# A mixture-of-experts feed-forward: a narrower path for experts with up to 192 tokens, and the weights fetched and split on an even schedule

## The chip, the cores and the metric

The program runs on one core of a Trainium2 chip. The metric is the device time of one execution in microseconds (us). The engines are named as the profile names them: PE multiplies matrices, PEld is PE's weight load, DVE and ACT are the vector and the scalar engine, POOL is the general-purpose engine, and SP issues most of the DMAs. An engine runs its own instructions in the order in which they are written and waits for others at semaphores.

## The reference

First a local and global attention over 8 batches of 544 rows, then a feed-forward layer in which a row is computed only where its skip score is positive, by the one of 8 experts that its gate picks.

```python
def reference(**kwargs):
    attn_out = _attn_ref(**attn_kwargs)          # (8, 8, 544, 64)
    x = attn_out.transpose(0, 2, 1, 3).reshape(B * S, H * D)    # (4352, 512)
    return _moe_ref(x=x, **moe_kwargs)

def _moe_ref(x, w_skip, w_gate, w1, w2):         # w1 (8, 512, 1024), w2 (8, 1024, 512)
    out = x.copy()
    do_compute = x @ w_skip > 0
    xc = x[do_compute]
    logits = xc @ w_gate
    e_idx = np.argmax(logits, axis=1)
    probs = softmax(logits)
    gate_w = probs[np.arange(len(xc)), e_idx]
    for e in range(8):
        mask = e_idx == e
        h = np.maximum(xc[mask] @ w1[e], 0.0)
        y[mask] = gate_w[mask, None] * (h @ w2[e])
    out[do_compute] = xc + y
```

With the inputs of the reference the experts 0 to 7 get 395, 171, 153, 289, 173, 371, 253 and 175 rows.

## The kernel before

The attention part fills the first half of the span and writes its rows (`x`) to the output in DRAM; it also appends each computed row's number and gate weight to a list of its expert in DRAM (`lst`). The change leaves it as it is. What follows is the expert part, lines 818 to 1040.

The order of every engine is written out by hand: the code runs under a manual schedule, so instructions stand on each engine as the Python emits them, and a "hook" after each step of a loop says what is slipped in there.

Each expert e handles its rows in a first group of 256 (`GRP`), and the rest, if any, in an extra group.

- `slots` reads the lists of row numbers and gate weights into `lt`, and `index` casts the numbers into `six`. In the first group, rows 2p and 2p+1 of the list go to partition p.
- `gather` (POOL, two indirect DMAs of 128 rows) fetches the rows: `xfirst` and `xsecond` in turn for the first groups, `xmore` for the extra ones.
- `turn_x` transposes them on PE (8 transposes of 128x128) and writes a high part `xh` (ACT) and the remainder `xl` (DVE): each float32 operand is used as a sum of two reduced-precision (`fp32r`) parts, so a product takes three matmuls: high x high, high x low, low x high.
- The up product (L858): for each of the 8 blocks `f` of 128 hidden units, 12 matmuls with 256 moving columns (4 of `w1h` with `xh`, 4 of `w1l` with `xh`, 4 of `w1h` with `xl`) into one of three PSUM banks `ph`; then ACT writes `hh` = relu(ph) and DVE the remainder `hlw`.
- The down product (L874): for each of the 2 token blocks `t` of 128 rows, 24 matmuls with 512 moving columns (per f: `hh` x `w2h`, `hh` x `w2l`, `hlw` x `w2h`) into a bank `py`. `put` then multiplies by the gate weight, adds the row (DVE, L939), and scatters the rows to the output (POOL, L940).
- The hook numbers 0 to 7 are the blocks of the up product, 8 to 15 those of the down product of t=0, 16 to 23 those of t=1.
- After the first group, `If(num > 256)` (L1010) holds the extra group: in full (L858 and L874 again) over 384 rows, else `ffn_half`, which does 128 rows another way (L904, L930). `num` is read from `cni` by all engines (L982).

Weights: expert e+1's two matrices (4 MB) come in 8 chunks of 512 KB (`raw`, six buffers); a `split` casts the chunk to its high part on ACT (L181) and subtracts on DVE (L184). Expert 1's first four chunks are issued on SP and the last four on POOL at hook 9 of expert 0, behind the gathers (`rest`); four of them are split in expert 0 at hooks 4 to 7, the other four in expert 1 at hooks 0 to 3, before expert 2's eight. In expert 1 and after it, the next expert's chunks are split at hooks 4, 5, 6, 8, 9, 11, 13, 15 (expert 1) or 0, 1, 2, 4, 5, 6, 9, 11.

## Time and profile before

| | |
|---|---|
| time, median of 3 runs | 499.26 us (497.95 to 500.41) |
| the profiled execution's own time | 503.73 us |
| its span | 502.0 us |
| mean granted PE clock | 0.986 |
| PE busy | 455.9 us (91%) |
| expert part: first up product to last scatter issued | 245.7 to 493.7 us |

The difference between the profiled execution's time and its span (1.7 us) lies around the program. Times inside the trace are counted from the span's start. A row of the timeline gives start, duration, engine, line, operation, output and inputs, shape and count, and in brackets the idle time of the engine just before it with what ended it. In a row of a window the busy time of each engine is followed by the number of its instructions, then the granted clock, the DMA engines' busy share and the GB/s that they moved.

### The profile page before, as it was taken

What the parts mean: (1) busy time and instruction counts of PE and PEld (TensorE: products, weight loads), DVE (VectorE), ACT (ScalarE), POOL (GpSimd) and SP (SyncE); (2) the same over time, 40 slices, a digit from 0 to 9 for tenths busy, and PEclk for the clock granted to TensorE, in tenths of its full rate; (3) what the DMA queues carried; (4) which work ended last, traced back from release to release, by engine and by line L of the source; (5) the groups of instructions that cost most, each with busy time, mean ns of one, the idle gap of its engine ahead of it and who ended that gap; (6) DMA issues with size and microseconds to landing.
All of it is one profiled execution on the core that took longest, in us unless ns stands there. A gap on an engine that the chain in (4) does not pass through costs nothing. (4 is left out here: it accounts for less than half of the span.)

```text
span 502.0 us, 13663 instructions
## 1 busy us (share of the span) xinstructions
PE 455.9 (91%) x4962; PEld 368.5 (73%) x4962; DVE 298.7 (59%) x1221; ACT 289.6 (58%) x883; POOL 228.2 (45%) x236
## 2 busy tenths in 40 slices
PE   8799999999989998887698999999989999899991
PEld 3576767776666767666696979898968888688881
DVE  6886767877757767784453229684714757047310
ACT  4689999899868887764341208563514545145210
POOL 6656666669864677776246014323202341013300
PEclk9999999999999999999899999999999999899996
DMA  8899898889957788610547308883820949113100
GB/s 252 267 329 262 268 288 279 254 281 219 289 171 244 226 189 255 169 45 2 172 146 216 109 26 268 313 295 121 286 99 10 343 142 327 38 23 131 46 15 17
DMA packets 50545, 93.32 MB, mean 186 GB/s; under 512 B 15596, under 2 KB 19948, under 8 KB 50448
## 3 DMA queue, kind: packets, MB, share of 16 engines
q1 hardware_dynamic: 44624, 81.83, 52.0%
q0 software_dynamic: 5824, 10.25, 6.2%
q8 instruction: 55, 0.90, 0.9%
q14 instruction: 42, 0.34, 0.3%
HBM read 82.91 MB, written 14.67 MB: 194 GB/s over the span
## 5 line engine op out<-in xcount | busy, mean ns | idle before, releaser
L368 ACT ACTIVATE prob<-prob,nmx 128x160 f32<-128x160 f32 x256 | 106.4, 418 | 17.9 <-DVE nmx L363 15.7
L398 POOL TENSOR_TENSOR prob<-prob,inv 128x640 f32<-128x640 f32 x64 | 80.3, 1257 | 61.1 <-DVE ing L428 24.0
L863 ACT ACTIVATE hh<-ph 128x256 fp32r<-128x256 f32 x72 | 27.7, 385 | 83.2 <-PE ph L858 71.8
L940 POOL DMA_INDIRECT out_dram<-yo,six x12 | 12.2, 1018 | 134.6 <-DVE yo L939 116.7
L874 PE MATMUL py<-w2h,hh 128*128 128x512 f32 x144 | 57.2, 397 | 0.0
L874 PE MATMUL py<-w2h,hlw 128*128 128x512 f32 x144 | 56.9, 395 | 0.0
L874 PE MATMUL py<-w2l,hh 128*128 128x512 f32 x144 | 56.7, 394 | 0.0
L351 PE MATMUL pss<-ks,qs 64*64 64x160 f32 x1024 | 51.5, 305 | 3.1 <-DVE nmx L363 1.6
L864 DVE SCALAR_TENSOR_TENSOR hlw<-ph,hh 128x256 fp32r<-128x256 f32 x72 | 30.3, 421 | 32.4 <-ACT hh L863 29.6
L351 PEld LDWEIGHTS pss<-ks,qs 64*64 64x64 f32 x1024 | 34.1, 134 | 20.9 <-issue 15.2
L858 PE MATMUL ph<-xh,w1h 128*128 128x256 f32 x288 | 46.4, 283 | 3.2 <-ACT xh L844 1.5
L482 PEld LDWEIGHTS pv<-ptT,vw 128*64 128x64 f32 x1024 | 39.4, 137 | 13.3 <-issue 3.9
L368 ACT ACTIVATION_READ_ACCUMULATOR prob<-prob,nmx 128x1 f32 x256 | 48.4, 189 | 0.0
L482 PE MATMUL pv<-ptT,vw 128*64 128x64 f32 (+1 forms) x1024 | 44.2, 237 | 3.4 <-ACT ptT L441 1.6
L858 PE MATMUL ph<-xh,w1l 128*128 128x256 f32 x288 | 45.5, 280 | 0.0
L858 PE MATMUL ph<-xl,w1h 128*128 128x256 f32 x288 | 45.4, 280 | 0.0
L858 PEld LDWEIGHTS ph<-xh,w1h 128*128 128x128 f32 x288 | 39.3, 191 | 5.9 <-issue 3.8
L639 POOL DMA_INDIRECT lst<-dat,slu x34 | 34.3, 1008 | 18.0 <-DVE cni L959 9.6
L858 PEld LDWEIGHTS ph<-xh,w1l 128*128 128x128 f32 x288 | 39.1, 190 | 0.0
L858 PEld LDWEIGHTS ph<-xl,w1h 128*128 128x128 f32 x288 | 39.0, 190 | 0.0
L438 PE MATMUL pst<-ident,prob 128*128 128x128 f32 x256 | 36.6, 281 | 2.5 <-POOL prob L398 1.2
L184 DVE TENSOR_TENSOR w1l<-raw,w1h 128x1024 fp32r<-128x1024 f32 x28 | 34.1, 1220 | 6.6 <-ACT w1h L181 4.1
(178 smaller groups left out, 942.3 us busy)
## 6 DMA issues: line engine op xcount, KB each, us to landing
raw<-in_w_dram SPq DMA_DIRECT2D x60, 512.0 KB
vw<-in_v_dram SPq DMA_DIRECT2D x32, 512.0 KB
ks<-in_kT_dram SPq DMA_DIRECT2D x32, 400.0 KB
out_dram<-xr SPq DMA_DIRECT2D x32, 256.0 KB
qs<-in_qT_dram SPq DMA_DIRECT2D x31, 256.0 KB
vgs<-in_vgl_dram SPq DMA_DIRECT2D x32, 64.0 KB
raw<-in_w_dram POOLq DMA_DIRECT2D x4, 512.0 KB
lst<-dat,slu POOLq DMA_INDIRECT x34
```

Of the source, the lines that this page charges most:

```text
L184: eng.tensor_sub(lo, raw, hi.bitcast(F32))
L351: nc.tensor.matmul(banks[odd][head(h ^ odd), j * W:(j + 1) * W], q[head(h), w * QB:(w + 1) * QB], window(k[head(h)], w), start=True, stop= ...
L368: nc.scalar.activation(pt[:, i, :], pt[:, i, :], AF.Exp, bias=nmx[:, i:i + 1], scale=-1.0, accum_out=sums[:, i, 0:1],)
L398: nc.gpsimd.tensor_mul(pt[:, sl, :], pt[:, sl, :], inv[:, sl].unsqueeze(2).to_broadcast([P, 4, W]),)
L438: nc.tensor.transpose(pst[:, i * P:(i + 1) * P], pt[:, 4 * hf + i, 0:KW], ident)
L482: nc.tensor.matmul(pv[head(h), j * 96:j * 96 + n], vv[:, w, head(h)], ptT[:, w, h ^ odd, 0:n], start=j == 0, stop=False, skip_group_check= ...
L639: ins = nc.gpsimd.indirect_dma_start(out=lst, out_offset=bass.IndirectOffsetOnAxis(ap=slu[:, t:t + 1], axis=0), in_=dat[:, bs[j], t - 4 * ...
L858: nc.tensor.matmul(ph[:, 0:GRP], hl[a][:, c, f * P:(f + 1) * P], bb[:, c, :], start=i == 0, stop=i == 3 * NC - 1,)
L863: nc.scalar.activation(hh[:, f, :], ph[:, 0:GRP], AF.Relu)
L864: nc.vector.scalar_tensor_tensor(hlw[:, f, :], ph[:, 0:GRP], 0.0, hh[:, f, :].bitcast(F32), ALU.max, ALU.subtract,)
L874: nc.tensor.matmul(py, a[:, f, ts_], hl[bb][:, f, :], start=f == 0 and i == 0, stop=f == NF - 1 and i == 2,)
L940: ins = nc.gpsimd.indirect_dma_start(out=out, out_offset=bass.IndirectOffsetOnAxis(ap=sidx, axis=0), in_=yo, in_offset=None, bounds_check= ...
```

## The change

It does four things.

1. **A path for up to 192 rows** (`FEW`). From expert 1 on, the up product stands twice, in the two arms of `If(nums[e] > FEW)` (L1128 of the changed kernel), and so does everything after the down product of t=0 (L1141). In the short arm `up_few` does a block f in 8 matmuls: 4 of `w1h` with 384 columns (192 of the high part and 192 of the low part side by side) and 4 of `w1l` with 192. ACT copies the second 192 columns, DVE adds them to the first, and relu and remainder are made from the sum, one block later. Rows 128 to 191 and their remainders then share one block of 128 stationary columns (POOL copies the remainders there, L1135), so that `down_few` does the second token block in 16 matmuls instead of 24, and `leave_few` adds the two halves: one ACT copy, and a second DVE instruction in `put`.
2. **The lists** are read so that rows 0 to 127 are token block 0: two DMAs with 8-byte pieces where one with 16-byte pieces was (experts 1 to 7).
3. **The weights** form one stream over all experts in six fixed buffers; a chunk is issued (`feed`) right after the split that frees a buffer. Expert 1's eight chunks are all split in expert 0 (hooks 4 to 7 and 17 to 20); chunks 4 to 7 are issued on ACT's queue (`early`, hooks 6 to 9) and no longer on POOL's behind the gathers. From expert 1 on the splits are at hooks 0, 2, ... 14; in `up_few` the second one's subtraction is done by POOL.
4. **The next expert's** rows are turned and its count is read at hook 15 and no longer at 16. The high and low parts are halves of one tile.

With the counts above, experts 1, 2, 4 and 7 take the short arms.

PE, where the up product of expert 1 stands; before, the last two of 8 blocks and the first matmul of the down product (`ph` is the result, `xh`, `xl` the rows' parts, `w1h`, `w1l` the weights' parts):

```order
L858 MATMUL ph<-xh_4453,w1h 128x256 x4
L858 MATMUL ph<-xh_4453,w1l 128x256 x4
L858 MATMUL ph<-xl_4454,w1h 128x256 x4
L858 MATMUL ph<-xh_4453,w1h 128x256 x4
L858 MATMUL ph<-xh_4453,w1l 128x256 x4
L858 MATMUL ph<-xl_4454,w1h 128x256 x4
L874 MATMUL py<-w2h,hh 128x512
```

The same place in the changed kernel: the end of the long arm, and the last two blocks of the short one (`x_4458` holds both parts).

```order
L864 MATMUL ph<-x_4458,w1l 128x256 x4
L864 MATMUL ph<-x_4458,w1h 128x256 x4
L1128 UNCONDITIONAL_BRANCH
L883 MATMUL ph<-x_4458,w1h 128x384 x4
L888 MATMUL ph<-x_4458,w1l 128x192 x4
...
L883 MATMUL ph<-x_4458,w1h 128x384 x4
L888 MATMUL ph<-x_4458,w1l 128x192 x4
L1128 UNCONDITIONAL_BRANCH
L916 MATMUL py<-w2h,h_4459 128x512
```

A block went from twelve rows of 256 columns to four of 384 and four of 192 in the short arm, and branches stand around both arms.

ACT in expert 0, from its sixth up block to the read of the counts; before:

```order
L863 ACTIVATE hh<-ph 128x256
L181 CAST w1h<-raw 128x1024
L863 ACTIVATE hh<-ph 128x256
L181 CAST w1h<-raw 128x1024
L863 ACTIVATE hh<-ph 128x256
L181 CAST w1h<-raw 128x1024
L982 TENSOR_LOAD cni
L844 CAST xh_4453<-xt 128x4x128 x2
```

The same place in the changed kernel, from the issue of the fifth chunk, ahead of the eighth up block's relu, on:

```order
L153 DMA raw_4451<-in_w_dram 128x2x512
L869 ACTIVATE h_4459<-ph 128x256
L188 CAST w1h<-raw_4450 128x1024
L153 DMA raw_4452<-in_w_dram 128x2x512
L153 DMA raw_4447<-in_w_dram 128x2x512
L153 DMA raw_4448<-in_w_dram 128x2x512
L188 CAST w2h<-raw_4451 128x1024
L188 CAST w2h<-raw_4452 128x1024
L188 CAST w2h<-raw_4447 128x1024
L188 CAST w2h<-raw_4448 128x1024
L1061 TENSOR_LOAD cni x2
L852 CAST x_4458<-xt 128x4x128 x2
```

Four DMA issues and four casts, each of which waits for its chunk, now stand ahead of the casts of expert 1's rows (`xt` to `x`).

The diff, cut to its core:

```diff
+Q = P // 2
+FEW = P + Q
 ...
     def slots(es, g):
-        if g == 0:
+        if g == 0 and es.start == 0:
             nc.sync.dma_start(
                 lt[:, es, 0].rearrange("p e t c -> p e (t c)"),
                 l3[es, 0:GRP, :].rearrange("e (p t) c -> p e (t c)", t=NSUB),
             )
         else:
             for t in range(NSUB):
+                n0 = g * GRP + t * P
                 nc.sync.dma_start(
-                    lt[:, es, 1, t],
-                    l3[es, GRP + t * P:GRP + (t + 1) * P, :].rearrange("e p c -> p e c"),
+                    lt[:, es, g, t], l3[es, n0:n0 + P, :].rearrange("e p c -> p e c")
                 )
 ...
+    def up_few(e, x2, hook, bank):
+        hl, late = wq[e], []
+        for f in range(NF):
+            ph = bank("ph")
+            fs = slice(f * P, (f + 1) * P)
+            for c in range(NC):
+                nc.tensor.matmul(
+                    ph[:, 0:2 * FEW], hl["w1h"][:, c, fs], x2[:, :, c, 0:FEW],
+                    start=c == 0, stop=False, skip_group_check=True,
+                )
+            for c in range(NC):
+                nc.tensor.matmul(
+                    ph[:, 0:FEW], hl["w1l"][:, c, fs], x2[:, 0, c, 0:FEW],
+                    start=False, stop=c == NC - 1, skip_group_check=True,
+                )
+            hs = fw.tile([P, DM], F32, name="yo")[:, 0:FEW]
+            nc.scalar.copy(hs, ph[:, FEW:2 * FEW])
+            nc.vector.tensor_add(hs, ph[:, 0:FEW], hs)
+            if late:
+                late.pop()()
+            def part(f=f, hs=hs):
+                h, lo = hh[:, f, 0:FEW], hlw[:, f, 0:FEW]
+                nc.scalar.activation(h, hs, AF.Relu)
+                nc.vector.scalar_tensor_tensor(
+                    lo, hs, 0.0, h.bitcast(F32), ALU.max, ALU.subtract
+                )
+            late.append(part)
+            if f == NF - 1:
+                late.pop()()
+            hook(f)
+    def down_few(e, hook, bank):
+        ...
+        for f in range(NF):
+            for i, bb in enumerate(("w2h", "w2l")):
+                nc.tensor.matmul(
+                    py, hh[:, f, P:GRP], hl[bb][:, f, :],
+                    start=f == 0 and i == 0, stop=f == NF - 1 and i == 1,
+                )
+            hook(2 * NF + f)
+        return py
+    def leave_few(py, xg, gate, sidx):
+        ys = fw.tile([P, DM], F32, name="ylast", bufs=1)
+        nc.scalar.copy(ys[0:Q], py[Q:P])
+        put(py, gate(1), xg[:, 1, :], sidx[:, 1:2], None, ys)
 ...
+        else:
+            gate, yo, sidx = gate[0:Q], yo[0:Q], sidx[0:Q]
+            nc.vector.scalar_tensor_tensor(yo, py[0:Q], gate, x[0:Q], ALU.mult, ALU.add)
+            nc.vector.scalar_tensor_tensor(yo, rest[0:Q], gate, yo, ALU.mult, ALU.add)
 ...
-            for _ in range(4):
-                weights[1].load(nc.gpsimd)
 ...
             if e + 1 < E:
                 load_weights(e + 1)
-                for _ in range(8 if e else 4):
-                    weights[e + 1].load()
+                for _ in range((4, 2, 0)[min(e, 2)]):
+                    feed()
 ...
             def split():
                 if e + 1 < E:
-                    weights[e + 1].split(nc.vector)
+                    w = weights[e + 1]
+                    w.split(nc.gpsimd if few and w.done % 4 == 1 else nc.vector)
+                    if e or w.done > NCH // 2:
+                        feed()
             if e == 0:
-                todo = {i: split for i in (4, 5, 6, 7)}
+                todo = {i: split for i in (4, 5, 6, 7, 17, 18, 19, 20)}
+                def early(i):
+                    if 6 <= i < 10:
+                        feed(nc.scalar)
             else:
-                todo = {i: split for i in (0, 1, 2, 4, 5, 6, 9, 11)}
-                todo[16] = nxt
+                todo = {i: split for i in range(0, 16, 2)}
+                todo[15] = nxt
 ...
+                with tc.If(nums[e] > FEW) as many:
+                    up(e, xs[e % 2], hook, ps_s)
+                with many.Else():
+                    up_few(e, xs[e % 2], hook, ps_s)
+                    nc.gpsimd.tensor_copy(hh[:, :, FEW:GRP], hlw[:, :, P:FEW])
+            put(down(e, 0, hook, ps_v), gate(0), xg[:, 0, :], sidx[:, 0:1])
+                with tc.If(nums[e] > FEW) as many:
+                    second()
+                with many.Else():
+                    leave_few(down_few(e, hook, ps_v), xg, gate, sidx)
```

## The prediction

> **What bounds the kernel now.** The page's first lines come first, then a table of windows cut at the steps of the expert part, then the timeline of PE.

> ```profile
> span 502.0 us, 13663 instructions
> PE 455.9 (91%) x4962; PEld 368.5 (73%) x4962; DVE 298.7 (59%) x1221; ACT 289.6 (58%) x883; POOL 228.2 (45%) x236
> L858 PE MATMUL ph<-xh,w1h 128*128 128x256 f32 x288 | 46.4, 283 | 3.2 <-ACT xh L844 1.5
> ```

> The third line tells which groups ran: a group of 256 rows issues 8 x 4 = 32 products of that kind, so 288 are nine groups: eight first groups and one full extra one.

> ```profile
> 274.65:285.96 11.31, 11.31 (x96) 11.31 (x97) 3.75 (x9) 2.69 (x7) 0.45 (x1) 1.00 0.45 162
> 285.96:297.20 11.24, 11.24 (x50) 8.83 (x48) 1.18 (x2) 0.38 (x1) 1.02 (x1) 1.00 0.07 25
> 298.29:309.67 11.38, 11.38 (x96) 11.38 (x97) 9.46 (x13) 9.15 (x14) 6.95 (x6) 1.00 0.55 174
> 309.67:322.10 12.43, 12.16 (x58) 9.71 (x57) 10.11 (x13) 6.60 (x9) 1.02 (x1) 1.00 0.97 354
> 470.00:492.00 22.00, 21.67 (x143) 19.35 (x141) 4.61 (x11) 3.07 (x8) 4.08 (x4) 1.00 0.07 23
> ```

> After length, the columns are PE, PEld, DVE, ACT and POOL busy, granted clock, DMA share, GB/s. The rows are expert 0's extra group (up, down), expert 1 (up; down with the turn of expert 2's rows) and expert 7. PE has no gap, at a full clock, and expert 1's up product takes the same time with DVE and ACT four fifths full as expert 0's with both idle. So PE sets the time here, and what leaves PE leaves the span, as long as the rest keeps up.

> ```profile
> 274.65 0.74 PE L858 MATMUL ph<-xh,w1h 128*128 128x256 f32 x4 [0.78 <-ACT xh L844]
> 285.96 0.40 PE L874 MATMUL py<-w2h,hh 128*128 128x512 f32 x1
> 296.92 0.40 PE L874 MATMUL py<-w2h,hlw 128*128 128x512 f32 x1
> 298.29 0.71 PE L858 MATMUL ph<-xh,w1h 128*128 128x256 f32 x4 [0.97 <-PEq L1016]
> 322.12 0.71 PE L858 MATMUL ph<-xh,w1h 128*128 128x256 f32 x4 [0.29 <-PEq L1010]
> ```

> Durations overlap, so starts count. A 256-column product steps by (285.96 - 274.65)/96 = 0.1178 us; a 512-column one by (296.92 - 285.96)/47 = 0.2332, or 0.456 ns a column (0.460 at 256).

> **The change part by part.** *Fewer products.* 384 columns lie between the two prices: 0.176. For 192 the floor by columns is 0.088; the ceiling is 0.118, since the same weights are loaded for 256 columns at that step. The nearest rows of narrow products:

> ```profile
> 244.42 0.63 PE L837 MATMUL xt<-ident,xfirst 128*128 128x128 f32 x4 [2.13 <-DMA xfirst<-out_dram,six]
> L837 PE MATMUL xt<-ident,xfirst 128*128 128x128 f32 x32 | 4.4, 274 | 3.2 <-DMA xfirst<-out_dram,six 3.2
> ```

> A 128-column transpose steps by (0.63 - 0.274)/3 = 0.119, twice its price by columns: narrow products are held up by something else. I take 0.110, near that row and inside the ceiling. The short up product is then 8 x (4 x 0.176 + 4 x 0.110) = 9.15 for 11.31, a saving of 2.16; the second token block drops 8 of 24 products, 8 x 0.2332 = 1.87. Four experts: 4 x 4.03 = -16.1 (-15.1 with the narrow step at 0.118, -18.9 at 0.088).

> [...] Whether loads or something else make the 0.119 no row here shows.

> *The evacuation of a short block.* Per block ACT has a copy and a relu of 192 columns where a relu was, DVE an addition and the remainder where a remainder was, and at each second block a split.

> ```profile
> L509 ACT COPY xT<-pv 128x256 f32<-128x256 f32 x64 | 20.3, 368 | 9.5 <-PE pv L501 9.4
> L441 ACT COPY ptT<-pst 128x512 f32<-128x512 f32 x32 | 18.2, 568 | 2.8 <-PE pst L438 2.8
> L863 ACT ACTIVATE hh<-ph 128x256 fp32r<-128x256 f32 x72 | 27.7, 385 | 83.2 <-PE ph L858 71.8
> L864 DVE SCALAR_TENSOR_TENSOR hlw<-ph,hh 128x256 fp32r<-128x256 f32 x72 | 30.3, 421 | 32.4 <-ACT hh L863 29.6 <-issue 1.5 <-ACTq L1016 1.0
> L181 ACT CAST w1h<-raw 128x1024 fp32r<-128x1024 f32 x28 | 29.2, 1044 | 0.3 <-DMA raw<-in_w_dram 0.3
> L184 DVE TENSOR_TENSOR w1l<-raw,w1h 128x1024 fp32r<-128x1024 f32 x28 | 34.1, 1220 | 6.6 <-ACT w1h L181 4.1 <-issue 1.5 <-DMA lst<-dat,slu 0.9
> ```

> A column of a copy costs (568 - 368)/256 = 0.78 ns, so 192 columns take 0.32, and I put the relu at 0.33. Two blocks cost ACT 2 x 0.32 + 2 x 0.33 + 1.04 = 2.34 and DVE, at about 0.33 for the addition and 0.36 for the remainder, 2 x 0.69 + 1.22 = 2.60, where PE needs 2 x 1.144 = 2.29. They are at PE's pace or just over, and the two hidden buffers `yo` make copy f+2 wait for remainder f. What pays is slack: three banks, and block 7 is first needed 4.9 us into the down product (7 x 3 x 0.233). If the engines pay whole durations, in this order with 0.06 per hand-over, PE loses 1.2 per expert; if neighbours overlap by 0.1, nothing. Experts 1, 2 and 4 have splits; expert 7 has none. I take 1.5 in all (0 to 4), the middle. `yo` is also what expert 3's extra group scatters just ahead of expert 4; that wait is within the 4.

> *Expert 0.* These rows are POOL's and SP's in expert 0, and PE's wait for the turned rows:

> ```profile
> 261.69 0.38 SPq L106 DMA_DIRECT2D lt<-lst  x1
> 262.12 1.50 SPq L112 DMA_DIRECT2D lt<-lst  x2
> 265.24 0.82 SPq L165 DMA_DIRECT2D raw<-in_w_dram  x2
> 265.78 1.05 POOL L119 DMA_INDIRECT xsecond<-out_dram,six  x1 [7.18 <-issue]
> 270.81 1.29 PE L837 MATMUL xt<-ident,xsecond 128*128 128x128 f32 x8 [1.35 <-DMA xsecond<-out_dram,six]
> 250.00:255.00 5.00, 5.00 (x52) 5.00 (x51) 2.27 (x11) 1.39 (x4) 2.25 (x3) 1.00 0.96 361
> ```

> Lists, then gathers, then PE: it already waits 1.35 and then 0.78 for the cast. Now the lists are one DMA more, with pieces of 8 bytes, and four chunks (2 MB) issued by ACT between hooks 6 and 9 move at the same time; at the last row's 361 GB/s these are 5.8 us. No row shows how lists and gathers share the engines with that. The low end is 0.5: the chunks end before the gathers, and the casts of the rows are only held up by the four splits ahead of them on ACT (4 x 1.04, most of it during the gathers). The high end is 6: the gathers come after all of the chunks. I take +2.5, less than half of the chunks, since the first are under way when the lists are read; range 0.5 to 6. The split of expert 1's last four chunks leaves expert 1 and so costs expert 0's extra group cover it has: DVE 3.75 of 11.31 is taken.

> *POOL and the stream.* In a short arm POOL does one subtraction of 1024:

> ```profile
> L184 POOL TENSOR_TENSOR w1l<-raw,w1h 128x512 fp32r<-128x512 f32 x8 | 10.2, 1270 | 0.0
> 352.71 1.16 POOL L119 DMA_INDIRECT xfirst<-out_dram,six  x1 [0.30 <-issue]
> 345.77 0.72 PE L858 MATMUL ph<-xh,w1h 128*128 128x256 f32 x4
> ```

> It takes 2 x 1.27 = 2.54 and stands behind the gathers, which end 8.1 after an expert's start (352.71 + 1.16 - 345.77), so its buffer and the chunk fed into it are some 10 us late. SP issues in order: later chunks wait behind that one. 4 MB take 11.6 us of a 20 us expert, so the cover holds by some us; if it does not, the next expert's first products wait. +0.5 (0 to 3). Moving the turn from hook 16 to 15 goes past nothing that waits: hook 15 is some 6 us after the gathers' end.

> *The end.* The last scatter waits for DVE:

> ```profile
> 491.71 0.75 DVE L939 SCALAR_TENSOR_TENSOR ylast<-py,lt,xsecond 128x512 f32<-128x512 f32 x1 [4.75 <-PE py L874]
> ```

> Now a copy on ACT (beside DVE's first) and a second such instruction: +0.75 (0.6 to 1.5).

> *The branches.* Seven experts pass two more `If`s, on all engines. PE's waits at the present ones are the 0.97 and 0.29 quoted. Both stand where an expert ends and a count is read; the new ones have their counts early and stand inside running work, between the same expert's products, so I take most as covered: +1 (0 to 13.6, each of 14 at 0.97).

> The sum: -16.1 + 1.5 + 2.5 + 0.5 + 0.75 + 1 = -9.85. The profiled execution's own time is 503.73 (span 502.0 and 1.7 around it), 4.5 above the median of 499.26. On its scale that gives 493.9; taken from the median, **489.4**.

> **The rivals.** *Exposed branches* (slower). Each way into or out of an arm halts the engine as at 298.29, whatever work surrounds it. The price is that row's 0.97, and 14 jumps cost 13.6, 12.6 more than counted: 489.4 + 12.6 = 502.0. It ends above before from ten of the fourteen on (-10.85 without any, 11 x 0.97 = 10.7). For it speaks the 0.97; against it the 0.29 at the next boundary, where PE passes the same kind of `If` with its condition false.

> [...]

> *The lists starve.* The 2 MB on ACT's queue go ahead of lists and gathers in full: 5.8 for what I put at 2.5, and the lists behind the same again: 489.4 + 5.8 = 495.2. For it speaks that PE waits for these gathers today, against it that 5.8 us of transfer, begun at 262, may end by the gathers' start.

> *Narrow fp32r products go at the price of plain float32.* No product of these two-part operands under 256 columns ran. Plain float32 has this row:

> ```profile
> 239.95 0.63 PE L531 MATMUL pr<-idw,xTg 128*128 128x137 f32 x4
> L531 PE MATMUL pr<-idw,xTg 128*128 128x137 f32 x16 | 2.6, 286 | 1.8 <-ACT xr L549 1.8
> ```

> Two records make a product there, (0.63 - 0.286)/3 = 0.115 each, so 137 columns take 0.23 or 1.68 ns a column. 192 then take 0.322, and 4 x 32 x (0.322 - 0.110) = +27.1: 516.5. Against it: 256 and 512 columns cost the same per column, so nothing begins to bend at 256.

> **How the numbers follow.** Forecast 0.70, branches 0.12, lists 0.10, narrow price 0.08. The forecast's own range is 481 to 496: all unknowns at their low ends give -18.9 + 0.5 + 0.6 = -17.8, or 481.5; upwards I let the evacuation and the lists go to their ends (+2.5 and +3.5). For 8 in 10 over all cases, 481 to 500: it takes in the lists and a part of the branches, and leaves out the narrow price. About 0.5% of 499, 2.5 us, is what a measurement can tell from no change. Faster: forecast and most of the lists, with a little of the branches, 0.76. Same: the branches around 499 to 501.8, 0.08. Slower 0.16.

> **What would show it.** In the changed profile PE's short up product should last 9.2 to 9.5 from its first 384-column product to the down product, and the second token block 16 x 0.233 = 3.7. A 192-column step over 0.2 would be the narrow price. DVE's idle time before its additions, and PE's waits for a bank in the short arms, show the evacuation. PE's waits for `xsecond` and for the cast in expert 0, 2.1 together now, should come to about 4.6; over 8 would be the lists. PE idle by its own queue at the new `If`s, each near 1, would be the branches. The forecast fails if expert 1 or 2 waits for chunks, or if the gain on PE returns as waits at these places.

## The result, and the profile after

The changed kernel takes 538.09 us (median of 4 runs, 537.07 to 541.97) where the kernel before takes 498.61 in the same comparison: a ratio of 1.0809 (95% interval 1.0736 to 1.0882), some 40 us slower. Forecast were 489.4 us, in a range of 481 to 500. Here and below a median is over all runs, while a ratio leaves out the executions that ran in a slower state (the profile of *fixed* is of one, so its expert part is left out).

The profiled execution took 537.24, its span is 535.4. The page's first lines:

```profile
span 535.4 us, 13599 instructions
PE 458.4 (86%) x4802; PEld 370.0 (69%) x4802; DVE 311.5 (58%) x1254; ACT 297.6 (56%) x919; POOL 234.9 (44%) x239
```

PE has 160 products fewer than before (4802 for 4962) and is busy 2.5 us longer: what it still does got slower. It also stands still where it did not; from PE's timeline, with the idle time in brackets:

```profile
274.21 1.94 PE L845 MATMUL xt<-ident,xsecond 128*128 128x128 f32 x8 [6.78 <-DMA xsecond<-out_dram,six]
306.55 1.62 PE L883 MATMUL ph<-x,w1h 128*128 128x384 f32 x4 [4.24 <-DMA out_dram<-yo,six]
312.74 0.88 PE L883 MATMUL ph<-x,w1h 128*128 128x384 f32 x4
313.46 0.59 PE L888 MATMUL ph<-x,w1l 128*128 128x192 f32 x4
313.88 0.87 PE L883 MATMUL ph<-x,w1h 128*128 128x384 f32 x4
329.08 0.47 PE L929 MATMUL py<-w2h,h 128*128 128x512 f32 x1 [2.86 <-issue]
340.74 0.96 PE L883 MATMUL ph<-x,w1h 128*128 128x384 f32 x4 [2.72 <-DVE yo L894]
359.08 0.47 PE L929 MATMUL py<-w2h,h 128*128 128x512 f32 x1 [2.66 <-issue]
427.07 0.47 PE L929 MATMUL py<-w2h,h 128*128 128x512 f32 x1 [2.36 <-issue]
502.70 0.94 PE L883 MATMUL ph<-x,w1h 128*128 128x384 f32 x4 [3.14 <-issue]
```

Four of these stops have nothing named behind them ("issue"): they stand at the entry of a short arm, three at its second part (L929), one at its first (502.70). Three more lie ahead of the extra groups of experts 3 and 5: 1.78 (389.74), 1.98 and 2.55 (457.84 and 460.79), where the kernel before has 0.88 and 1.08. The rows from 312.74 on are the undisturbed step: (313.46 - 312.74)/4 = 0.18 for 384 columns, (313.88 - 313.46)/4 = 0.105 for 192.

The windows of expert 1, of the stretch behind its entry at 329.08, and of expert 7 (columns as before; the granted clock stands third from the end):

```profile
306.55:334.43 27.88, 24.33 (x112) 21.43 (x113) 16.91 (x26) 12.95 (x26) 8.68 (x7) 0.83 0.53 172
329.08:332.50 3.42, 3.42 (x9) 2.70 (x10) 2.48 (x4) 0.00 (x0) 0.66 (x1) 0.56 0.89 280
502.70:523.08 20.38, 20.38 (x104) 18.14 (x104) 5.90 (x17) 4.76 (x16) 2.99 (x4) 0.92 0.06 18
```

Expert 1 takes 27.88 for 23.83 before, though it has fewer products; behind the stop that ends at 329.08 the granted clock is 0.56 over 3.42 us. Summed over windows of 1 us in the expert part, 1 less the granted clock comes to 24.0 us (3.1 before), a part of it while PE stands.

Counted from one expert's first up product on PE to the next one's, the experts 0 to 6 last 63.4, 27.9, 30.1, 40.2, 27.6, 43.7 and 26.6; before, they last 52.6, 23.8, 23.7, 37.4, 23.6, 39.2 and 23.6. Expert 7's PE work takes 20.4 for 22.1: it alone gained.

### The profile page after: what moved, and what is told of

Read it like the earlier page. It is cut to its first block, busy times and chain, and to the rows that moved or that the text cites. A ratio compares the mean times of both kernels' runs of the same rounds, so it can differ in the third digit from the quotient of the medians.

```text
span 535.4 us, 13599 instructions
## 1 busy us (share of the span) xinstructions
PE 458.4 (86%) x4802; PEld 370.0 (69%) x4802; DVE 311.5 (58%) x1254; ACT 297.6 (56%) x919; POOL 234.9 (44%) x239
## 5 line engine op out<-in xcount | busy, mean ns | idle before, releaser
L999 POOL DMA_INDIRECT out_dram<-yo,six x16 | 16.1, 1003 | 140.2 <-DVE yo L994 109.3
L916 PE MATMUL py<-w2h,h 128*128 128x512 f32 x224 | 73.5, 400 | 0.3
L916 PEld LDWEIGHTS py<-w2h,h 128*128 128x128 f32 x224 | 42.2, 190 | 10.6 <-DVE w1l L191 1.6
L864 PE MATMUL ph<-x,w1h 128*128 128x256 f32 x320 | 46.6, 286 | 1.4 <-ACT x L852 0.7
L358 PEld LDWEIGHTS pss<-ks,qs 64*64 64x64 f32 x1024 | 33.5, 133 | 19.2 <-issue 12.3
L883 PE MATMUL ph<-x,w1h 128*128 128x384 f32 x128 | 34.1, 395 | 13.2 <-DVE yo L894 5.7
L916 PE MATMUL py<-w2l,h 128*128 128x512 f32 x112 | 44.5, 397 | 0.0
L864 PEld LDWEIGHTS ph<-x,w1h 128*128 128x128 f32 x320 | 42.3, 194 | 2.3 <-ACT x L852 2.0
L893 ACT COPY yo<-ph 128x192 f32<-128x192 f32 x32 | 10.2, 319 | 60.1 <-PE ph L888 41.1
L188 ACT CAST w2h<-raw 128x1024 fp32r<-128x1024 f32 (+1 forms) x36 | 32.3, 948 | 13.5 <-DVE six L104 8.6
L883 PEld LDWEIGHTS ph<-x,w1h 128*128 128x128 f32 x128 | 25.3, 225 | 15.2 <-issue 8.2
L191 DVE TENSOR_TENSOR w2l<-raw,w2h 128x1024 fp32r<-128x1024 f32 x28 | 32.6, 1221 | 4.4 <-ACT w2h L188 4.4
L445 PEld LDWEIGHTS pst<-ident,prob 128*128 128x128 f32 x256 | 28.2, 143 | 9.3 <-issue 4.8
```

What stands on the lines that cost most here:

```text
L188: nc.scalar.copy(hi, raw)
L191: eng.tensor_sub(lo, raw, hi.bitcast(F32))
L358: nc.tensor.matmul(banks[odd][head(h ^ odd), j * W:(j + 1) * W], q[head(h), w * QB:(w + 1) * QB], window(k[head(h)], w), start=True, stop= ...
L445: nc.tensor.transpose(pst[:, i * P:(i + 1) * P], pt[:, 4 * hf + i, 0:KW], ident)
L864: nc.tensor.matmul(ph[:, 0:GRP], hl[a][:, c, f * P:(f + 1) * P], x2[:, part, c, :], start=i == 0, stop=i == 3 * NC - 1,)
L883: nc.tensor.matmul(ph[:, 0:2 * FEW], hl["w1h"][:, c, fs], x2[:, :, c, 0:FEW], start=c == 0, stop=False, skip_group_check=True,)
```

## The experiments

Ratios are to the kernel before in the same comparison. "Expert part" is PE's time in the profiled execution from expert 0's first up product to PE's end; it leaves out the attention, whose end lies up to 10 us apart between profiles. Each kernel has one profile.

| kernel | median us | ratio (95%) | expert part |
|---|---|---|---|
| before | 499.26 | 1 | 245.9 |
| changed | 538.09 | 1.081 (1.074 to 1.088) | 280.0 |
| all_long | 518.82 | 1.036 (1.030 to 1.043) | 264.0 |
| both_long | 528.87 | 1.053 (1.046 to 1.061) | 275.8 |
| static | 512.90 | 1.025 (1.019 to 1.030) | 257.9 |
| swap_out | 537.49 | 1.075 (1.070 to 1.081) | 284.2 |
| all_long_hooks | 506.65 | 1.015 (1.008 to 1.021) | 253.4 |
| all_long_late | 517.03 | 1.038 (1.030 to 1.045) | 263.1 |
| both_long_hooks | 528.23 | 1.052 (1.042 to 1.062) | 271.6 |
| one_if | 534.09 | 1.068 (1.062 to 1.074) | 277.8 |
| tiny_if | 513.11 | 1.020 (1.013 to 1.028) | 255.1 |
| long_old | 505.30 | 1.006 (1.003 to 1.009) | 246.5 |
| static_hs | 510.61 | 1.020 (1.011 to 1.030) | 251.8 |
| static_old | 509.43 | 1.012 (1.007 to 1.017) | 249.1 |
| no_tail_feed | 509.90 | 1.023 (1.019 to 1.027) | 256.1 |
| after_dve | 536.82 | 1.075 (1.068 to 1.082) | 279.0 |
| static_hs_dve | 494.19 | 0.992 (0.988 to 0.995) | 238.6 |
| best_static | 503.76 | 1.009 (1.006 to 1.012) | 246.5 |
| fixed | 531.05 | 1.057 (1.051 to 1.063) | |
| fixed_one | 519.79 | 1.037 (1.034 to 1.040) | 259.5 |

**Taking the change apart.** *all_long*: no short arms and no new branches.

```diff
-                with tc.If(nums[e] > FEW) as many: ... many.Else(): up_few(...)
+            up(e, xs[e % 2], hook, ps_s)
-                with tc.If(nums[e] > FEW) as many: second() ... many.Else(): leave_few(...)
+            second()
```

> The changed kernel without its short arms and without the new branches: every expert takes the long path in straight code, while the new fetch, the lists and the splits stay. Theory (the loss is PE's stops: late gathers in expert 0, the entries and exits of the new arms, a shared buffer): expert 0 keeps its 10.9 us, the rest is as before, so 506 to 511. Rival (the new fetch is harmless and expert 0's stops belong to the branches behind it): 497 to 501.

The time, 518.8, is above both ranges. Expert 0 lasts 62.8 (there the theory is right), but new stops also stand at the ends of experts 1, 2 and 4 (2.53, 1.50, 1.50), where nothing but the old branch lies.

*both_long*: the branches, with the long code in both arms.

```diff
-                    up_few(e, xs[e % 2], hook, ps_s)
+                    up(e, xs[e % 2], hook, ps_s)
-                    leave_few(down_few(e, hook, ps_v), xg, gate, sidx)
+                    py = down(e, 1, hook, ps_v); put(py, gate(1), ..., yl)
```

> The changed kernel with the new branches, but the long code in both of their arms, so that the branches stand alone. Theory: seven experts pay an entry or exit of 2.4 to 3.1 us plus about 2 us of halved clock: 25 to 33 above the straight long kernel, 533 to 541. Rival (the branches are covered by queued work, and the short arms' own work is slow): within 7 us of the straight long kernel.

The branches cost 10 us (8.5 by the ratios), between the two forecasts. The stops of all_long at the ends of experts 1, 2 and 4 are gone, and others stand at the new branches (4.23, 1.39, 3.24, 2.39): the extra group's code lies inside one arm of the second branch, so that an expert in the other arm jumps once there and not twice.

*static*: short paths chosen at build time for experts 1, 2, 4 and 7.

```diff
-                with tc.If(nums[e] > FEW) as many:
+            if e not in (1, 2, 4, 7): up(...)
+            else: up_few(...)
```

> The changed kernel with the path of each expert chosen when the program is built (experts 1, 2, 4 and 7 short), no branch around either product. Theory: four short experts save 4.0 each on PE against the straight long kernel and lose up to 6 at the shared buffer: 495 to 503. Rival (the narrower products or their evacuation are slow in themselves): 508 or more.

It takes 512.9, 25 below the changed kernel (28 by the ratios), so the changed kernel's branches cost that much; but it is only 6 below all_long, where 16 were to be saved. The rival's number is right: without any branch, the short path as it stands loses most of its gain.

*swap_out*: the last output in `ylast`, the helper copy in `yo`.

```diff
-        ys = fw.tile([P, DM], F32, name="ylast", bufs=1)
+        ys = fw.tile([P, DM], F32, name="yo")
-        put(py, gate(1), xg[:, 1, :], sidx[:, 1:2], None, ys)
+        put(py, gate(1), xg[:, 1, :], sidx[:, 1:2], yl, ys)    # yl: the tile ylast
```

> The changed kernel, only that in the short arm the last output is made in the tile ylast and the helper copy in the tile yo, the other way round than now, so that the scatter in flight no longer holds the buffer that the next short up product fills first. Theory: expert 2's stops of 2.72 and 0.69 go, with about 2 us of halved clock: 4 to 6 faster than the changed kernel, 532 to 535. Rival (the copy waits for older scatters or for the branch anyway): 537 to 539.

No change. The copy now waits for the other scatter; ACT's timeline in expert 2, of the changed kernel and then of swap_out:

```profile
339.98 0.32 ACT L893 COPY yo<-ph 128x192 f32<-128x192 f32 x1 [4.72 <-DMA out_dram<-yo,six]
```

```profile
343.99 0.32 ACT L893 COPY yo<-ph 128x192 f32<-128x192 f32 x1 [4.70 <-DMA out_dram<-ylast,six]
```

The copy still has its tile in common with scatters. Why it waits for one out of `ylast` the trace does not show; waits at a branch that cover both arms could do it, which no run tried by itself. A tile of its own took the wait away, with built-in paths (static_hs, below) and with branches (in fixed_one 0.34 is left at this place).

**The even hooks.** *all_long_hooks*: splits back at the early hooks.

```diff
-                todo = {i: split for i in range(0, 16, 2)}
+                todo = {i: split for i in (0, 1, 2, 4, 5, 6, 9, 11)}
```

> The straight long kernel with the splits of the next expert's chunks back at hooks 0, 1, 2, 4, 5, 6, 9 and 11, so that no chunk is in flight where an expert ends. Theory: PE's stops at the skipped extra groups (2.53, 1.50 and 1.50 by PE's own queue, with DMA engines 0.5 to 1.0 busy just before, and none at the boundary without weights) come from the evenly spread transfers: they fall to 0.3 or less, 511 to 514 for 518.8. Rival (the jump itself costs that, whatever the DMA engines do): 517 to 520.

It is 12 us faster (11 by the ratios), more than expected: the stops at the ends of experts 1 and 2 are gone; one of 1.31 is left at the end of expert 4. *no_tail_feed* keeps the even hooks and leaves out half of the later experts' weights, the half that was fetched late.

```diff
-                        feed()
+                        feed(None if e and w.done > 4 else nc.sync)    # None: nothing is fetched
```

> The straight long kernel with even hooks (518.8), in which from expert 1 on the splits at hooks 8 to 14 stay but fetch no chunk behind them: half of the weights of the later experts is not fetched anew, so its time stands for no whole computation. Theory (PE stops at the skipped extra groups because the weights in flight delay the fetch of code): the stops of 1.5 to 2.5 go although the splits stand where they did, 505 to 510. Rival (the late splits on ACT and DVE make the stops): 516 to 521.

It takes 509.9, as the theory had it, and after expert 0 no stop at an expert's end is left. From expert 1's first product to PE's end all_long takes 201.2 us, all_long_hooks 190.1 and no_tail_feed 189.3, so there the whole loss of the even hooks comes back; by the ratios it is only 6.8 of 10.9, as expert 0, which this edit leaves alone, lasted 66.8 in this profile and 62.8 in all_long. The same boundary in all_long (PE's row, then two windows) and in no_tail_feed (the row has no bracket: no stop):

```profile
330.31 1.19 PE L864 MATMUL ph<-x,w1h 128*128 128x256 f32 x4 [2.53 <-PEq L1118]
326.00:327.00 1.00, 1.00 (x6) 0.82 (x5) 0.00 (x0) 0.00 (x0) 0.00 (x0) 1.00 1.03 395
328.00:329.00 1.00, 0.00 (x0) 0.00 (x0) 0.56 (x1) 0.00 (x0) 0.16 (x1) 1.00 0.09 29
```

```profile
331.81 0.71 PE L864 MATMUL ph<-x,w1h 128*128 128x256 f32 x4
```

Just ahead of the jump the DMA engines move 395 GB/s (the last but one column is their share, 1.03); PE then stands until after they are idle. Without weights in flight the same jump shows no stop, and weights spread evenly to an expert's last third meet the jump at its end. But busy DMA engines alone do not make the stop. In the kernel before, expert 2's first product waits only 0.29 at this jump (322.12), with as much in flight just ahead of it:

```profile
321.00:322.00 1.00, 0.83 (x4) 0.35 (x2) 0.13 (x1) 0.00 (x0) 0.02 (x1) 1.00 0.95 363
```

And the 1.31 that is left in all_long_hooks begins with the DMA engines nearly idle (it starts at 410.39, and their share from 410 to 411 is 0.07). What else it takes stays open.

**The branches.** *both_long_hooks*: both_long with the hooks' line of all_long_hooks.

> The kernel with the long code in both arms of the new branches, with the splits at the early hooks. Theory (a jump stops the engines only where its target has to be fetched while weights fill the DMA engines): it comes to within 4 us of the straight long kernel with early hooks, 511 to 517. Rival (the jumps cost their 10 us in any case): 520 to 524.

The time is above both ranges, on the rival's side: 528.2 is 21.6 above all_long_hooks, 1.5 a branch. At three of its entries (stops of 1.54, 2.11 and 3.69) weights are still in flight: the DMA share is 1.00 from 329 to 330 in the first, 0.95 and 0.93 in the two microseconds from 354 on in the second, and 1.04 from 417 to 418 in the third. At the entry of expert 7, which has no next weights to fetch, the branch stops PE all the same, with the DMA engines at 0.17 and 64 GB/s over the stop:

```profile
491.20 0.92 PE L864 MATMUL ph<-x,w1h 128*128 128x256 f32 x4 [3.06 <-issue]
488.14:491.20 3.06, 0.01 (x1) 0.00 (x0) 0.75 (x1) 0.00 (x0) 1.68 (x2) 1.00 0.17 64
```

*tiny_if* has as many branches at the same places, around one small instruction:

```diff
+            if e:
+                with tc.If(nums[e] > FEW):
+                    nc.vector.memset(lt2, 0.0)
```

> The straight long kernel with early hooks (506.7), with two extra branches per expert from expert 1 on, at the places of the new ones, around one small memset of an unused tile instead of a whole product. The compared counts, the engines and the number of branches are those of the changed kernel, but what is skipped is a few instructions long. Theory (the stop is the fetch of code that lies far from the branch): 505 to 510. Rival (a branch stops every engine by itself): 520 to 530, as with the long code in both arms.

By the ratios it is 0.6% (2.8 us) above all_long_hooks, 0.2 a branch, which the two intervals cannot tell from nothing; both_long_hooks is 3.7% above. PE's dearest entry in both_long_hooks, and a row of tiny_if right after its branch:

```profile
420.35 0.80 PE L916 MATMUL py<-w2h,h 128*128 128x512 f32 x1 [3.69 <-issue]
```

```profile
335.76 0.73 PE L864 MATMUL ph<-x,w1h 128*128 128x256 f32 x4 [0.48 <-PEq L1118]
```

A branch that skips a few instructions (a near one, from here on) was nearly free here (0.2), one that skips a product (a far one) was not (1.5). The small branch also does away with any waits that large arms bring along, so this pair alone does not show that the stop is the fetch of the target's instructions. The trace of the changed kernel has a DMA queue that its page calls "instruction", q8: 58 packets, 0.95 MB, so 16 KB each, one per 9 us on average. These are the DMA queues in the stops that end at 329.08 and at 502.70, and then in the stop at the shared buffer that ends at 340.74 (packets, MB, share of the 16 engines' time):

```profile
q1 hardware_dynamic: 131, 0.50, 56.8%
q8 instruction: 1, 0.02, 2.5%
```

```profile
q0 software_dynamic: 53, 0.22, 16.5%
q8 instruction: 1, 0.02, 2.3%
q14 instruction: 1, 0.01, 0.6%
```

```profile
q0 software_dynamic: 48, 0.09, 14.4%
```

Each of the changed kernel's six stops over 2 us at a branch (4.24, 2.86, 2.66, 2.36, 2.55, 3.14) has such a packet, which begins between 0.2 us before the stop and 1.4 us into it, and PE goes on 1.4 to 1.9 us after the packet's end. The stop of 2.72 at the shared buffer has none. By the queue's name, code is fetched in these stops; that its arrival is what ends them is inferred, and no run shows it by itself. A packet alone does not make a stop: in the kernel before, one lies from 345.65 to 346.53 at the jump ahead of expert 3, and PE goes on there at 345.77, after 0.14. Whether the stops of 1.50, 1.50, 1.31 and 2.53 at the old branch in all_long and all_long_hooks hold a packet of q8 is not shown here.

*one_if*: one branch around all of an expert.

```diff
+                with tc.If(nums[e] > FEW) as many:
+                    up(...); put(down(e, 0, ...)); second()
+                with many.Else():
+                    up_few(...); put(down(e, 0, ...)); leave_few(...)
```

> The changed kernel with one branch per expert around everything (up, down and output) in place of two, the counts read ahead of it. Theory: the stops of 2.86, 2.66 and 2.36 at the entry of the second short arm go, each with 1.5 to 2 us of halved clock: 523 to 528 for 538. Rival (the stop only moves to the entry or the exit of the longer arm): 534 or more.

It saves only 4 us (6.4 by the ratios): three stops at L929 went, but longer ones stand at the first product of experts 1, 4 and 7 (6.33, 3.26, 4.93). That is the rival's number, and mostly its reason.

**Expert 0.** *all_long_late*: chunks 4 to 7 on POOL behind the gathers, split at hook 23.

```diff
             gather(xmore, six[:, 0, 1, :])
+            for _ in range(4): feed(nc.gpsimd)
-                    if 6 <= i < 10: feed(nc.scalar)
-                todo = {i: split for i in (4, 5, 6, 7, 17, 18, 19, 20)}
+                todo = {i: split for i in (4, 5, 6, 7)}; todo[23] = last    # four splits
```

> The straight long kernel with the second expert's chunks 4 to 7 no longer on ACT's queue but issued on POOL behind the gathers in expert 0, and split at its last hook. Theory: the list writes, list reads and gathers no longer share the DMA engines with them, PE's wait for xsecond falls from 7.6 to 1.5 to 3 and expert 0 from 62.8 to 53 to 56: 509 to 512 for 518.8. Rival (the lists' smaller pieces make the delay): 515 or more.

At 517.0 it has the rival's number, but not for the rival's reason: the waits moved. PE's rows there:

```profile
269.20 1.06 PE L845 MATMUL xt<-ident,xsecond 128*128 128x128 f32 x8 [2.45 <-DMA xsecond<-out_dram,six]
280.58 1.23 PE L864 MATMUL ph<-x,w1h 128*128 128x256 f32 x4 [8.68 <-ACT x L852]
```

The gathers came in time (2.45 for 7.64), and then the cast of the extra group's rows stood on ACT behind four splits that waited for their chunks. *long_old* splits these chunks in expert 1, as before, and turns the next expert's rows at hook 16 again.

```diff
-                todo[23] = last
+                if e == 1: todo.update({i: own for i in range(4)})    # the four splits
+                todo = {i: split for i in ((0, 1, 2, 4, 5, 6, 9, 11) if e > 1 else (4, 5, 6, 8, 9, 11, 13, 15))}
```

> The straight long kernel with the old schedule of the second expert's chunks: 4 to 7 issued on POOL behind the gathers, split in expert 1 at hooks 0 to 3, the other splits where they were; lists and tiles stay new. Theory (what is left of the loss, 7.5, is expert 0's fetch): 498 to 502. Rival (the lists' smaller pieces): 504 or more.

Its median, 505.3, is out of the theory's range, but the kernel before ran at 502.84 beside it: it is 0.6% above, and the expert part is 246.5 for 245.9. So, against the 253.4 of all_long_hooks, expert 0's fetch makes 6.9 of the expert part. That the lists and tiles seem to add next to nothing is a balance: in these profiles expert 0 still lasts 55.7 for 52.6 (PE waits 1.85 and 0.98 for `xsecond` where it waited 1.35), and the rest is 2.6 shorter. Where the fetch begins to show (changed kernel):

```profile
255.38 1.23 POOL L646 DMA_INDIRECT lst<-dat,slu  x1 [0.30 <-issue]
255.58 0.42 ACTq L153 DMA_DIRECT2D raw<-in_w_dram  x1
263.29 2.21 SPq L115 DMA_DIRECT2D lt<-lst  x4
```

From the last list write to the reads of the lists it takes 7.9 us; before, 4.4 (its last list write starts at 257.33). Two chunks issued by ACT stand right behind that write; with them gone it is 5.0 in all_long_late and 4.5 in long_old.

**The short path without branches.** *static_hs*: static with early hooks and the helper copy in a tile of its own.

```diff
-            hs = fw.tile([P, DM], F32, name="yo")[:, 0:FEW]
+            hs = fw.tile([P, FEW], F32, name="hs", bufs=2)
```

> The path chosen when the program is built, the splits at the early hooks, and the helper copy of the short up product in a tile of its own instead of the shared yo. Theory: 512.9, less 12 for the hooks, less 5 to 7 for the stops at the shared buffer in experts 2 and 4 and their halved clock: 493 to 497. Rival (the evacuation itself is too slow): 500 or more.

The rival's number: against all_long_hooks the short products now save 1.6 us of the expert part. (In this and all later runs with `hs`, three small tiles of the routing have one buffer in place of two, which was not tried by itself.) *static_old* has long_old's edit too.

> As the kernel before in this list, with the old schedule of the second expert's chunks too: the narrower products without any of the stops. By the prediction's term (4.03 per short expert) it should stand 16 below the straight long kernel with that schedule, less 0 to 4 for the evacuation: 482 to 489. Rival (twelve splits beside the short products of expert 1 hold PE up): 490 to 495.

It is above both ranges. In both kernels DVE is late; expert 4 in static_hs, DVE and POOL:

```profile
402.91 6.24 DVE L191 TENSOR_TENSOR w2l<-raw,w2h 128x1024 fp32r<-128x1024 f32 x1
403.36 2.41 POOL L191 TENSOR_TENSOR w1l<-raw,w1h 128x1024 fp32r<-128x1024 f32 x1
405.72 2.34 POOL L191 TENSOR_TENSOR w2l<-raw,w2h 128x1024 fp32r<-128x1024 f32 x1
```

A subtraction of 1.22 takes 6.24: it ends 1.1 after the second of POOL's two, as if it had run behind both. In expert 2 of the changed kernel:

```profile
344.72 2.38 POOL L191 TENSOR_TENSOR w1l<-raw,w1h 128x1024 fp32r<-128x1024 f32 x1
344.89 0.36 DVE L894 TENSOR_TENSOR yo<-ph,yo 128x192 f32<-128x192 f32 x1 [0.79 <-ACT yo L893]
345.16 2.16 DVE L901 SCALAR_TENSOR_TENSOR h<-yo,h 128x192 fp32r<-128x192 f32 x1
```

The addition, which reads one operand from PSUM, passes; the remainder (L901), which reads two from SBUF, ends 0.22 after POOL's end (347.10): it takes 2.16 for 0.35. Beside POOL's subtractions in experts 1 and 4 a remainder takes 2.17 and 2.43. That POOL's instruction holds it is inferred from these times. *after_dve* and *static_hs_dve* give the subtraction back to DVE:

```diff
-                    w.split(nc.gpsimd if few and w.done % 4 == 1 else nc.vector)
+                    w.split(nc.vector)
```

> The changed kernel with the one subtraction that POOL does in each short up product given back to DVE. Theory (while POOL subtracts 1024 columns, DVE's instruction beside it stands still, 0.35 becoming 2.16 in expert 2, and the same 3.82 for 1.22 in the kernel with built-in paths): DVE loses 2.4 and wins 1.2 to 1.9 in each of experts 1, 2 and 4, so 532 to 537 for 538. Rival (DVE is the fuller engine, and the work returned to it delays PE more): 539 to 543.

> The kernel with built-in paths, early hooks and the helper copy in its own tile (510.6), with POOL's two subtractions per short expert given back to DVE. Theory: DVE's instruction of 6.24 in expert 4 falls back to 1.2 and PE's wait of 3.82 there with its halved clock goes, as do the waits of 1.2 in experts 1 and 2: 502 to 507. Rival (six splits in eight short blocks are too many for DVE alone): 509 to 514.

In the changed kernel this gives 1.3 us (2.8 by the ratios), which the intervals cannot tell from nothing. With built-in paths, where POOL has two subtractions per short expert, it is 2.9% by the ratios (14 us): 494.2, 0.8% below the kernel before (0.992, 0.988 to 0.995), and better than expected. Experts 1 and 7 of static_hs_dve, and then the same in all_long_hooks (the first number behind the window is its length):

```profile
305.37:325.65 20.28, 19.94 (x112) 17.67 (x113) 16.65 (x28) 13.05 (x26) 7.58 (x7) 1.00 0.65 212
462.57:481.14 18.57, 18.57 (x104) 16.56 (x104) 6.47 (x18) 4.78 (x16) 4.73 (x5) 1.00 0.08 29
```

```profile
303.71:326.86 23.15, 23.00 (x152) 20.66 (x153) 14.91 (x21) 11.65 (x18) 7.86 (x7) 1.00 0.65 222
471.70:493.83 22.13, 22.13 (x144) 19.81 (x144) 4.79 (x10) 3.07 (x8) 4.08 (x4) 1.00 0.08 27
```

*best_static*: static_hs_dve with long_old's edit and other hooks.

```diff
-                todo = {i: split for i in ((0, 1, 2, 4, 5, 6, 9, 11) if e > 1 else ...)}
+                todo = {i: split for i in ((0, 2, 4, 6, 8, 9, 10, 11) if e > 1 else ...)}
```

> Built-in paths, helper copy in its own tile, no subtraction on POOL, the old schedule of the second expert's chunks, and the later experts' splits at hooks 0, 2, 4, 6, 8, 9, 10 and 11. Theory: with every stop found so far out of the way, the short products keep most of their 4.03 per expert: PE's expert part, 246.5 in the straight long kernel with that schedule, falls to 232 to 238, and the time to 491 to 497. Rival (the evacuation takes the saving back in any order): expert part 242 or more, 501 or more.

It has the rival's number, but not by the evacuation: the late hooks bring back stops ahead of the extra groups (2.51 and 2.02), and expert 2 waits 2.65 for its turned rows behind expert 1's twelve splits.

**The repairs with the branches.** *fixed* is the changed kernel with the three edits of static_hs_dve (early hooks, `hs`, DVE); *fixed_one* has one branch per expert besides.

> The changed kernel with its branches, and the three repairs that made the built-in paths fast (494.2): early hooks, the helper copy in its own tile, no subtraction on POOL. What stands between the two is then the far branches alone. Theory (two far branches per expert cost what they cost with the long code in both arms, 18 us of PE's expert part): 509 to 517. Rival (the shorter code of the short arms makes them cheap, or the repairs took their stops away too): 497 to 504.

> The same three repairs, with one branch per expert around everything. Theory: half the far jumps, 9 to 12 us above the built-in paths, 502 to 507, still not below the kernel before. Rival (the longer jump costs as much as two): 509 or more.

They take 531.0 and 519.8: by the ratios the branches cost 32 and 22 us on a kernel whose other stops were repaired, 2.3 and 3.2 each, more than any theory had. The short paths would be worth their place only if they could be reached without a far branch: static_hs_dve is a little faster than before, but its paths are fixed for these counts, so it is no replacement.

## Why the prediction was wrong, point by point

In steps, by the ratios and 499 us, the loss is made up of lists and tiles +2.8 (long_old), expert 0's fetch +4.4 (all_long_hooks), even hooks +10.9 (all_long), short paths -5.8 (static), and branches +28 (changed), together +40. The first is uncertain by 1.5 us, each later difference by 3 to 5. By the expert parts of one profile each the steps are +0.6, +6.9, +10.6, -6.1 and +22.1, together +34. The order matters, since stops hide one another.

- **The narrower products (-16.1): right.** 0.105 and 0.18 a step for 0.110 and 0.176, which rules out the rival of the plain float32 price. With the stops of the short path gone, the expert part falls by 14.7 from all_long_hooks to static_hs_dve (253.4 to 238.6), where this term and the evacuation come to 14.6; it is 3.6 in expert 7 and 2.9 in expert 1.
- **The branches (+1): the step that failed most.** The argument was that jumps inside running work are covered. tiny_if bears that out for near targets (0.2 each); far ones cost 1.5 to 3.2 each, where the rival's dearest case had 0.97, the one row that showed such a wait. That rival had the place and the sign, at a chance of 0.12, and a third to two thirds of the price. (By its own figures, 10.85 over 0.97 each, it ends above the kernel before from twelve jumps on, not from ten.)
- **POOL and the stream (+0.5, 0 to 3): failed twice.** Even hooks cost 10.9, by stops at an expert's end that went when the late weights did; the prediction had looked for late chunks only. And POOL's subtraction was priced by its own length, 2.54, not by what it does to DVE: 1.81 lost in one instruction of expert 2, and 14 us between static_hs and static_hs_dve, which differ by two such subtractions per short expert. In the changed kernel itself, with one, it is not clear of noise.
- **The evacuation (+1.5, 0 to 4): too low for another reason than priced.** The engines' work fits (static_hs_dve), but the shared `yo` held PE for 2.72 and 0.69 in expert 2, as well as for 1.07 and 0.70 in expert 4, the only one for which the prediction had named it.
- **Expert 0 (+2.5, 0.5 to 6): undersized.** Expert 0 lasts 63.4 for 52.6. Of these 10.8, 3.3 stand at the entry to expert 1 (4.24 for 0.97); 7.5 are left, above the range and near the 8.3 (2.5 and 5.8) of the rival of the starved lists, and the fetch makes 6.9 of them by long_old. PE's waits for `xsecond` and the cast, forecast at 4.6 together, are 7.5 (6.78 and 0.68). The list writes, which neither had, are delayed as well.
- **The end (+0.75): undersized.** From PE's last product to the span's end it takes 12.3, before 10.3: +2.0, above the range of 0.6 to 1.5.
- **No term for the clock.** The same 4802 products keep PE busy for 458.4 in the changed kernel and, in static_hs_dve,

```profile
PE 439.2 (89%) x4802; PEld 354.7 (72%) x4802; DVE 307.2 (62%) x1257; ACT 298.5 (61%) x919; POOL 229.4 (47%) x236
```

  Most of the 19 us between them is the halved clock behind stops: 1 less the granted clock, times PE's busy time, comes to some 21 us in the expert part of the one and 5 in the other.
- **The first product of expert 1 (4.24)** is a stop that no step had. The profile names the extra group's scatter, but a packet of q8 that ends at 304.68 lies in it too. In static and all_long the same place costs 0.97, in both_long 4.23, so it comes with the branch; which of the two makes it was not tried by itself.

## What to carry to other kernels

Before a path is put behind a branch, price the branch by what it skips: near ones cost 0.2 here, far ones 1.5 to 3.2, and two of them about as much as the 4 us that the path saved, or more. When transfers are spread, look at what stands at the end of the stretch that they now reach, and when work goes to POOL, at what DVE does beside it. Where the clock falls after a stop of PE, count what it loses too: 3.4 us at half the clock are 1.7.
